# Weight splitting spread out and its copies put off by a step, the MLP begun three steps later, and the squares of the first chunk shared by two engines

## The chip, the core and the metric

The kernel runs on one core of a Trainium2 chip. The metric is device time in microseconds (us) of one execution. The engines named below are TensorE (PE; its weight loads are PEld), VectorE (DVE), ScalarE (ACT), GpSimd (POOL, which here only issues transfers) and SyncE (SP, which only issues transfers). Each engine runs its own instructions in the order in which the program gives them, and waits at the first whose operands or target are not ready.

## What is computed

```python
scores = (1.0 / S) * np.matmul(z, z.transpose(0, 2, 1))   # z: 4 x 3008 x 64
attn = np.maximum(scores, 0.0) ** 2
x = (u * np.matmul(attn, v)).reshape(B * S, D)            # u, v: 4 x 3008 x 256
h = x @ w_in                                              # 256 x 2048
g = h * np.clip(h + 3.0, 0.0, 6.0) / 6.0
y = g @ w_out                                             # 2048 x 256
```

All in float32; the two weights arrive as 64-bit floats.

## The kernel before, in words

**Precision.** Every operand of a matmul is split into a high part, rounded to the type that TensorE multiplies (a copy, cast or square, mostly on ScalarE), and a low part, the rest (a subtraction on VectorE). A product is then three matmuls: high by high, high by low, low by high.

**Steps.** A batch has 6 chunks of 512 columns (the last one 448), and a chunk takes 12 pairs of row tiles; one pass of the inner loop, numbered g from 0 to 287, is a *step* and handles one pair. In a step `attend` multiplies pair g with v (12 matmuls into the two banks o0 and o1), while `scores` prepares pair g + 2: four matmuls (s), two Relu evictions on ScalarE (L367), the square (`r2`), its rounded high part (`ah`) and its low part (`al`, L73). Scores are symmetric. A pair that was computed already for another chunk is read back from DRAM, transposed on VectorE (L318, `rm`) and split, which takes no score matmuls. I call such a pair mirrored and the others direct. Squares that a later chunk needs are written to DRAM by `keep`. In the first chunk the full-precision square is a VectorE multiplication (L384); in chunks 1 to 3 it is a second ScalarE square (L382). At a chunk's end two VectorE multiplications (L440) form x from u and the banks o0, o1.

**Weights.** `weight_ops` is a generator. For each of 16 weight blocks (in0, out0, in1, out1, ... out7) it decodes the 64-bit floats in seven VectorE operations (`to_f32`), for an "in" block forms four sums `s`, then queues ScalarE copies for the high parts into the tile `wb`, subtracts the low parts on VectorE (L73 wb) and writes `wb` to DRAM (L183, `dwin`, `dwout`). There is one buffer `wb`. `weight_work` takes `build_rate(g)` yields of the generator in each step, in `background()`. The queued copies are put into ScalarE's program by `flush_copies`, which `scores` and `from_mirror` call, and which the builder itself calls before its subtractions.

**MLP.** A *group* (m = 0 to 95) multiplies one block of x with one in/out block pair: 7 products of 3 matmuls (m; Strassen's scheme, tiles `ra`, `hb`, `rb`) and 24 matmuls (y). A group spans three steps, from step `MLP_FROM` on; the groups that are left after step 287 run back to back in a last loop. At its start a group reads block m + 1 of w_in and block m of w_out back from DRAM (`fetch_w`, L194: `wi`, `wo`). Its results are split into `gh0`, `gl0`, `gh1`, `gl1` of `gpool`, which nothing uses before the first group. `split_x` splits a block of x (6 VectorE low parts and sums of 512 or 1024 columns) in the three steps before the block's first group, and then `load_u` (L432) fetches the next u into the one buffer.

**Queues.** All hardware transfers are issued by SP in program order: `keep` (L304), reads of mirrored pairs (L287), weight writes (L183) and reads (L194), `load_u`. GpSimd issues the raw weights (L101, `wraw`).

Of the kernel before, what the change touches and what calls it, by code (L numbers as in the profile page):

```python
# [7 lines left out]
F32 = mybir.dt.float32  # L8
U32 = mybir.dt.uint32
F32R = mybir.dt.float32r  # L10
AF = mybir.ActivationFunctionType
ALU = mybir.AluOpType
# [3 lines left out]
P = 128  # L16
CH = 512
# [5 lines left out]
NFP = NF // 2  # L23
NPR = B * NCH // 2

MLP_FROM = 30
EVERY = 3
AFTER = MLP_FROM - 27

# [7 lines left out]
def relu2_attention_then_hswish_mlp(  # L37
# [9 lines left out]
    nc = tc.nc  # L47
# [18 lines left out]
    def f(ap):  # L66
        return ap.bitcast(F32)
# [4 lines left out]
    def sub(out, a, b):  # L72
        nc.vector.tensor_tensor(out=out, in0=a, in1=b, op=ALU.subtract)  # L73

    def add(out, a, b):
        nc.vector.tensor_tensor(out=out, in0=a, in1=b, op=ALU.add)  # L76
# [8 lines left out]
    wide = w_in.shape[-1] == 2 * DFF  # L85

    copies = []

    def flush_copies():
        while copies:  # L90
            copies.pop(0)()

    raws = {}

    def fetch_raw(kind, q):
        cols = slice(q * 2 * P, q * 2 * P + 2 * P) if kind == "in" else slice(0, D)
        src = w_in if kind == "in" else w_out[q * 2 * P:q * 2 * P + 2 * P]
        src = src.rearrange("(k p) f -> p k f", p=P)
        if wide:
            raw = rpool.tile([P, 2, D, 2], U32, tag="r", name="wraw")  # L100
            nc.gpsimd.dma_start(  # L101
                out=raw.rearrange("p k n w -> p k (n w)"),
                in_=src[:, :, 2 * cols.start:2 * cols.stop],
            )
        else:
            raw = rpool.tile([P, 2, D], F32, tag="r", name="wraw")
            nc.gpsimd.dma_start(out=raw, in_=src[:, :, cols])
        raws["w", kind, q] = raw
# [33 lines left out]
        return f0  # L142

    dw = {}

    def build(kind, q, then):

        raw = raws.pop(("w", kind, q))
        if wide:
            w = yield from to_f32(raw)  # L150
        else:
            w = raw
        then()
        if kind == "in":
            s = stg.tile([P, 4, P], F32, tag="stg", name="s4")
            t = wpool.tile([P, 2, 7, P], F32R, tag="wb", name="wb")
            a11, a21 = w[:, 0, :P], w[:, 0, P:]
            a12, a22 = w[:, 1, :P], w[:, 1, P:]
            add(s[:, 0], a21, a22)
            copies.append(lambda: nc.scalar.copy(out=t[:, 0, A11:A22], in_=w[:, :, :P]))  # L160
            copies.append(lambda: nc.scalar.copy(out=t[:, 0, A22], in_=a22))
            yield
            sub(s[:, 1], s[:, 0], a11)
            yield
            sub(s[:, 2], a11, a21)
            yield
            sub(s[:, 3], a12, s[:, 1])
            copies.append(lambda: nc.scalar.copy(out=t[:, 0, S1:], in_=s))
            yield
            flush_copies()  # L170
            sub(t[:, 1, A11:A22], w[:, :, :P], f(t[:, 0, A11:A22]))
            yield
            sub(t[:, 1, A22], a22, f(t[:, 0, A22]))
            yield
            sub(t[:, 1, S1:], s, f(t[:, 0, S1:]))
        else:
            t = wpool.tile([P, 2, 2, D], F32R, tag="wb", name="wb")
            copies.append(lambda: nc.scalar.copy(out=t[:, 0], in_=w))
            yield
            flush_copies()  # L180
            sub(t[:, 1], w, f(t[:, 0]))
        d = dw[kind, q] = dwpool.tile(list(t.shape), F32, tag=f"{kind}{q}", name=f"dw{kind}")
        nc.sync.dma_start(out=d, in_=f(t))  # L183
        yield

    def fetch_w(kind, q):
        while (kind, q) not in dw:
# [159 lines left out]

        return t.rearrange("p r n -> p (r n)").rearrange("p (q m e) -> p m q e", q=4, m=8)

    def scores(b, c, p, square_on_act=False, banks="xx"):  # L350


        if p // 2 < c:
            yield from from_mirror(b, c, p)
            return
        n = width(c)
        zx, zy = (z[:, :n] for z in zt[b, c])
        rt = rpool.tile([P, 2, CH], F32, tag="r", name="rt")
        rn = rt[:, :, :n]
        for r in range(2):  # L360
            s = ps.tile([P, CH], F32, tag=banks[r], name="s")
            j = 2 * p + r
            cols = slice((j % 4) * P, (j % 4) * P + P)
            zj = zt[b, j // 4][0][:, cols]
            mm(s[:, :n], zj, zy, True, False)
            mm(s[:, :n], zj, zx, False, True)
            nc.scalar.activation(out=rn[:, r], in_=s[:, :n], func=AF.Relu, scale=1.0 / S)  # L367
            if not r:
                yield
        ah = apool.tile([P, 2, CH], F32R, tag="ah", name="ah")  # L370
        al = apool.tile([P, 2, CH], F32R, tag="al", name="al")
        hn, ln = ah[:, :, :n], al[:, :, :n]
        keeps = p // 2 > c
        r2, r_of, r2_of, h_of, l_of = rn, rn, rn, f(hn), ln
        if keeps or not square_on_act:
            r2 = r2_of = rpool.tile([P, 2, CH], F32, tag="r", name="r2")[:, :, :n]
        if keeps:
            r_of, r2_of = in_order(rn), by_quadrant(r2)
            h_of, l_of = in_order(f(hn)), in_order(ln)
        if square_on_act:  # L380
            nc.scalar.activation(out=hn, in_=rn, func=AF.Square)
            nc.scalar.activation(out=r2_of, in_=r_of, func=AF.Square)  # L382
        else:
            nc.vector.tensor_tensor(out=r2_of, in0=r_of, in1=r_of, op=ALU.mult)  # L384
            nc.scalar.activation(out=hn, in_=rn, func=AF.Square)  # L385
        flush_copies()
        if keeps:
            keep(b, c, p, r2)
        yield
        if p < NPAIR - 1:  # L390
            sub(l_of, r2_of, h_of)
        else:
            first, second = (slice(0, 4), slice(4, 8)) if keeps else (0, 1)
            to = in_order(hn) if keeps else hn
            sub(l_of[:, first], r2_of[:, first], h_of[:, first])
            sub(to[64:128, second], r2_of[64:128, second], h_of[64:128, second])
        at[b, c, p] = (ah, al)
        yield
# [202 lines left out]
    def weight_ops():  # L601
        fetch_raw(*weights[0])
        yield
        for n, w in enumerate(weights):
            yield from build(*w, lambda: n + 1 < len(weights) and fetch_raw(*weights[n + 1]))

    w_ops = weight_ops()

    def build_rate(g):
        return 0 if g < 6 else 2 if g < 12 else 5 if g < MLP_FROM else 4  # L610

    def weight_work(n):
        for _ in range(n):
# [19 lines left out]
    with tc.manual_schedule():  # L633
# [16 lines left out]
        for i, (b, c) in enumerate(chunks):  # L650
            ahead = b + 1 if c == NCH - 1 and b + 1 < B else None
            for p in range(NPAIR):
                g = i * NPAIR + p
                pair = pairs[g]
                if i == 0:
# [6 lines left out]
                    if p % 2 == 0 and p // 2 + 2 < NCH:  # L662
                        split_z(0, p // 2 + 2)
                at_mlp, on = divmod(g - MLP_FROM, EVERY)
                if at_mlp < 0:
                    unit = iter(())
                elif on == 0:
                    unit = group(at_mlp)
                if g + 2 < len(pairs):
                    nxt = scores(*pairs[g + 2], square_on_act=0 < i < 4, banks="xy" if at_mlp < 0 else "yx" if on == 2 else "yy")  # L670
                else:
                    nxt = iter(())
                g_done = min(g + 3, len(pairs))
# [138 lines left out]
```

## Time and profile before

| | |
|---|---|
| three runs | 1972.79, 1974.31 (median), 1980.26 us |
| the profiled execution | 1977.08 us |
| its span, first to last instruction | 1975.3 us |
| mean granted TensorE clock | 0.994 |
| PE busy | 1911.7 us (97%), 8400 matmuls |
| DVE busy | 1520.2 us (77%) |
| ACT busy | 1195.8 us (61%) |

Busy time is what the profile counts as an instruction running; matmuls overlap one another, so a busy PE is not a PE at its peak. "Idle before" an instruction is the time in which its engine had nothing running, and the name behind the arrow is what ended it.

### The profile page before, as it was taken

The page shows a single profiled execution, that of the slowest core. Times are in us where ns is not written, and L with a number is a line of the kernel's source. Part 1 is how long each engine was busy: PE and PEld are TensorE (multiplying, and loading weights), DVE is VectorE, ACT ScalarE, POOL GpSimd, SP SyncE. Part 2 cuts the span into 40 slices and gives each one's busy share as a digit, 9 for nine tenths or more (in the row PEclk, how much of TensorE's full clock was granted, in tenths as well). Part 3 has the DMA queues.
Part 4 walks back from the last instruction along what each step waited for, and adds up shares of the span by engine and source line. Part 5 has one row for each costly group of instructions (what it writes and reads, how often), then busy time and mean ns, then how long its engine had stood idle before and what let it go on. Part 6 is the DMA issues. An engine that isn't in the chain of part 4 may idle for free.

```text
span 1975.3 us, 23141 instructions
## 1 busy us (share of the span) xinstructions
PE 1911.7 (97%) x8400; PEld 1578.3 (80%) x8400; DVE 1520.2 (77%) x1762; ACT 1195.8 (61%) x1632; POOL 54.2 (3%) x88
## 2 busy tenths in 40 slices
PE   7878999999999999999999999999999999999998
PEld 5656777888888888888888888888888888888877
DVE  7888897887767767887767776878876787787675
ACT  6566656566555655567655655557665565564565
POOL 1000000010000000011000000001000000000000
PEclk9998999999999999999999999999999999999999
DMA  7877667746544555675635546576455464557243
GB/s 190 230 205 230 173 200 202 194 150 185 177 131 123 160 154 146 186 194 142 213 113 149 163 126 167 139 197 181 139 183 143 139 182 123 152 161 196 85 145 117
DMA packets 416177, 325.02 MB, mean 165 GB/s; under 512 B 252608, under 2 KB 375488, under 8 KB 416064
## 3 DMA queue, kind: packets, MB, share of 16 engines
q1 hardware_dynamic: 408704, 299.96, 53.6%
q0 software_dynamic: 7360, 23.60, 4.3%
q8 instruction: 66, 1.08, 0.2%
q14 instruction: 47, 0.39, 0.1%
HBM read 239.34 MB, written 84.15 MB: 164 GB/s over the span
## 4 chain that ended last, share of the span: by engine, by line
PE 77%; DVE 10%; ACT 5%; DMA 5%; issue 3%; SPq 1%; DVEq 0%; ACTq 0%; POOLq 0%
PE o L70 29%; PE y L70 22%; PE m L70 20%; PE s L70 6%; DVE rm L318 1%; DVE r L384 1%; DMA l<-d 1%; DVE xl L73 1%; ACT rt L367 1%; DVE al L73 1%; DVE rb L541 1%; DMA wo<-dwout 1%; SPq L287 1%; DMA d<-r 1%; DMA wraw<-in_w_in_dram 1%
## 5 line engine op out<-in xcount | busy, mean ns | idle before, releaser
L70 PE MATMUL y<-gh,wo 128*128 128x512 f32 (+1 forms) x1536 | 531.0, 387 | 3.6 <-DMA wo<-dwout 3.6
L70 PE MATMUL m<-xh,wi 128*128 128x512 f32 (+1 forms) x1344 | 493.0, 389 | 12.9 <-ACT rt L367 5.8
L70 PE MATMUL o<-ah,vl 128*128 128x512 f32 (+1 forms) x1152 | 447.6, 389 | 10.9 <-DVE u L440 5.0
L70 PE MATMUL o<-ah,vh 128*128 128x512 f32 (+1 forms) x1152 | 446.5, 388 | 0.0
L70 PE MATMUL o<-al,vh 128*128 128x512 f32 (+1 forms) x1104 | 428.7, 388 | 9.3 <-DVE al L73 9.3
L70 PEld LDWEIGHTS y<-gh,wo 128*128 128x128 f32 x1536 | 288.8, 188 | 59.9 <-issue 3.3
L70 PEld LDWEIGHTS m<-xh,wi 128*128 128x128 f32 x1344 | 252.8, 188 | 73.2 <-ACT rt L367 10.4
L70 PE MATMUL y<-gl,wo 128*128 128x512 f32 (+1 forms) x768 | 298.0, 388 | 2.5 <-DVE gl L73 2.3
L367 ACT ACTIVATE rt<-s 128x512 f32<-128x512 f32 x336 | 195.5, 595 | 125.2 <-PE s L70 124.5
L384 DVE TENSOR_TENSOR r<-rt 128x1024 f32<-128x1024 f32 (+1 forms) x145 | 175.5, 1210 | 116.5 <-ACT rt L367 116.1
L70 PEld LDWEIGHTS o<-ah,vl 128*128 128x128 f32 x1152 | 217.7, 189 | 59.0 <-DVE u L440 4.9
L70 PE MATMUL m<-xl,wi 128*128 128x512 f32 (+1 forms) x672 | 260.3, 387 | 0.7 <-DVE xl L73 0.7
L70 PEld LDWEIGHTS o<-al,vh 128*128 128x128 f32 x1104 | 208.7, 189 | 52.9 <-DVE al L73 11.6
L70 PEld LDWEIGHTS o<-ah,vh 128*128 128x128 f32 x1152 | 217.5, 189 | 41.5
L76 DVE TENSOR_TENSOR hb<-hb,m 128x512 f32<-128x512 f32 (+1 forms) x192 | 129.1, 672 | 106.9 <-PE m L70 105.3
L573 ACT ACTIVATE ra<-m,three 128x512 f32<-128x512 f32 (+1 forms) x96 | 65.3, 681 | 218.9 <-PE m L70 210.1
L73 DVE TENSOR_TENSOR al<-r,ah 128x1024 fp32r<-128x1024 f32 (+2 forms) x163 | 185.1, 1136 | 12.0 <-ACT r L382 10.1
L70 PEld LDWEIGHTS y<-gl,wo 128*128 128x128 f32 x768 | 144.4, 188 | 33.9 <-DVE gl L73 6.9
L73 DVE TENSOR_TENSOR gl<-rb,gh 128x1024 fp32r<-128x1024 f32 (+1 forms) x96 | 115.3, 1201 | 55.1 <-ACT gh L80 54.0
L385 ACT ACTIVATE ah<-rt 128x1024 fp32r<-128x1024 f32 (+1 forms) x145 | 153.2, 1057 | 4.6
L70 PE MATMUL s<-zy,zx 128*128 128x512 f32 x336 | 134.3, 400 | 19.5 <-DVE zx L73 11.9
L70 PEld LDWEIGHTS m<-xl,wi 128*128 128x128 f32 x672 | 126.5, 188 | 23.5 <-DVE xl L73 1.0
(69 smaller groups left out, 2166.8 us busy)
## 6 DMA issues: line engine op xcount, KB each, us to landing
wi<-dwin SPq DMA_DIRECT2D x96, 896.0 KB, 5.9
d<-r SPq DMA_DIRECT2D x220, 256.0 KB, 3.3
wo<-dwout SPq DMA_DIRECT2D x96, 512.0 KB, 6.7
l<-d SPq DMA_DIRECT2D x320, 128.0 KB, 3.4
l<-d SPq DMA_DIRECT2D x160, 112.0 KB, 3.3
vraw<-in_v_dram POOLq DMA_DIRECT2D x33, 256.0 KB, 4.1
u<-in_ut_dram SPq DMA_DIRECT2D x8, 1024.0 KB, 5.5
out_dram<-y SPq DMA_DIRECT2D x16, 512.0 KB, 4.9
```

The source lines that it names most:

```text
L70: nc.tensor.matmul(out, lhsT=lhsT, rhs=rhs, start=start, stop=stop, skip_group_check=part)
L73: nc.vector.tensor_tensor(out=out, in0=a, in1=b, op=ALU.subtract)
L76: nc.vector.tensor_tensor(out=out, in0=a, in1=b, op=ALU.add)
L287: nc.sync.dma_start(out=t[32 * q:32 * q + 32, :nk, :], in_=src[:, c0:c0 + 64].rearrange("(k e) f -> e k f", e=32),)
L318: nc.vector.transpose(out=rn.rearrange("p r (k e) -> p r k e", e=32), in_=t[:, :n // 32].rearrange("p k (r e) -> p r k e", r=2),)
L367: nc.scalar.activation(out=rn[:, r], in_=s[:, :n], func=AF.Relu, scale=1.0 / S)
L384: nc.vector.tensor_tensor(out=r2_of, in0=r_of, in1=r_of, op=ALU.mult)
L385: nc.scalar.activation(out=hn, in_=rn, func=AF.Square)
L541: nc.vector.scalar_tensor_tensor(out=out, in0=out, scalar=6.0, in1=h, op0=ALU.min, op1=ALU.mult)
L573: nc.scalar.activation(out=ra[:, 1], in_=c21, func=AF.Relu, bias=three)
```

## The change

Four things are altered. (1) A queued copy remembers its step (`now`), and `flush_copies` puts it into ScalarE's program only in a later step; only `finish`, which subtracts the low parts, flushes everything. `finish` of a block now runs after the seven decode operations of the next block. (2) High and low part have a tile each and are written to DRAM by a transfer each. Until step 30 the blocks take turns on three pairs of tiles (`wh`/`wl`, and the idle `gh0`/`gl0` and `gh1`/`gl1`), from step 31 on all use `wh`/`wl`. (3) The MLP begins at step 33 and not 30, which moves `split_x` and `load_u` by three steps too and leaves 11 groups, not 10, for the last loop; the generator is called at other rates. (4) In the first chunk VectorE squares the first half of a pair and ScalarE the second ("da"); chunks 1 to 3 ("aa") and the rest ("dd") are as before.

```diff
@@ -23,7 +23,7 @@
 NFP = NF // 2
 NPR = B * NCH // 2
 
-MLP_FROM = 30
+MLP_FROM = 33
 EVERY = 3
 AFTER = MLP_FROM - 27
 
@@ -85,10 +85,15 @@
     wide = w_in.shape[-1] == 2 * DFF
 
     copies = []
-
-    def flush_copies():
-        while copies:
-            copies.pop(0)()
+    now = -1
+
+    def copy_later(out, of):
+        copies.append((now, out, of))
+
+    def flush_copies(upto=None):
+        while copies and (upto is not None or copies[0][0] < now):
+            _, out, of = copies.pop(0)
+            nc.scalar.copy(out=out, in_=of)
 
     raws = {}
 
@@ -142,46 +147,66 @@
         return f0
 
     dw = {}
-
-    def build(kind, q, then):
-
-        raw = raws.pop(("w", kind, q))
-        if wide:
-            w = yield from to_f32(raw)
+    early = True
+
+    def pieces(kind, w):
+
+        hi, lo = piece_tiles(kind)
+        if kind == "out":
+            copy_later(hi, w)
+            return [(hi, lo, w)]
+        s = stg.tile([P, 4, P], F32, tag="stg", name="s4")
+        a11, a21 = w[:, 0, :P], w[:, 0, P:]
+        a12, a22 = w[:, 1, :P], w[:, 1, P:]
+        copy_later(hi[:, A11:A22], w[:, :, :P])
+        copy_later(hi[:, A22], a22)
+        add(s[:, 0], a21, a22)
+        yield
+        sub(s[:, 1], s[:, 0], a11)
+        yield
+        sub(s[:, 2], a11, a21)
+        yield
+        sub(s[:, 3], a12, s[:, 1])
+        copy_later(hi[:, S1:], s)
+        yield
+        return [
+            (hi[:, A11:A22], lo[:, A11:A22], w[:, :, :P]),
+            (hi[:, A22], lo[:, A22], a22),
+            (hi[:, S1:], lo[:, S1:], s),
+            hi, lo,
+        ]
+
+    def finish(kind, q, parts):
+        if kind == "out":
+            hi, lo = parts[0][:2]
         else:
-            w = raw
-        then()
-        if kind == "in":
-            s = stg.tile([P, 4, P], F32, tag="stg", name="s4")
-            t = wpool.tile([P, 2, 7, P], F32R, tag="wb", name="wb")
-            a11, a21 = w[:, 0, :P], w[:, 0, P:]
-            a12, a22 = w[:, 1, :P], w[:, 1, P:]
-            add(s[:, 0], a21, a22)
-            copies.append(lambda: nc.scalar.copy(out=t[:, 0, A11:A22], in_=w[:, :, :P]))
-            copies.append(lambda: nc.scalar.copy(out=t[:, 0, A22], in_=a22))
+            *parts, hi, lo = parts
+        flush_copies(upto=now)
+        for h, l, of in parts:
+            sub(l, of, f(h))
             yield
-            sub(s[:, 1], s[:, 0], a11)
-            yield
-            sub(s[:, 2], a11, a21)
-            yield
-            sub(s[:, 3], a12, s[:, 1])
-            copies.append(lambda: nc.scalar.copy(out=t[:, 0, S1:], in_=s))
-            yield
-            flush_copies()
-            sub(t[:, 1, A11:A22], w[:, :, :P], f(t[:, 0, A11:A22]))
-            yield
-            sub(t[:, 1, A22], a22, f(t[:, 0, A22]))
-            yield
-            sub(t[:, 1, S1:], s, f(t[:, 0, S1:]))
-        else:
-            t = wpool.tile([P, 2, 2, D], F32R, tag="wb", name="wb")
-            copies.append(lambda: nc.scalar.copy(out=t[:, 0], in_=w))
-            yield
-            flush_copies()
-            sub(t[:, 1], w, f(t[:, 0]))
-        d = dw[kind, q] = dwpool.tile(list(t.shape), F32, tag=f"{kind}{q}", name=f"dw{kind}")
-        nc.sync.dma_start(out=d, in_=f(t))
-        yield
+        d = dw[kind, q] = dwpool.tile([P, 2, *hi.shape[1:]], F32, tag=f"{kind}{q}", name=f"dw{kind}")
+        for k, t in enumerate((hi, lo)):
+            nc.sync.dma_start(out=d[:, k], in_=f(t))
+
+    built = []
+
+    def piece_tiles(kind):
+        homes = (("wh", "wl"), ("gh0", "gl0"), ("gh1", "gl1")) if early else (("wh", "wl"),)
+        tags = homes[len(built) % len(homes)]
+        built.append(kind)
+        tiles = []
+        for tag in tags:
+            if tag[0] == "g":
+                t = gpool.tile([P, 2, CH], F32R, tag=tag, name=tag)
+                t = t.rearrange("p r n -> p (r n)")
+            else:
+                t = wpool.tile([P, 7 * P], F32R, tag=tag, name=tag)
+            if kind == "in":
+                tiles.append(t[:, :7 * P].rearrange("p (m f) -> p m f", m=7))
+            else:
+                tiles.append(t[:, :2 * D].rearrange("p (r d) -> p r d", r=2))
+        return tiles
 
     def fetch_w(kind, q):
         while (kind, q) not in dw:
@@ -347,7 +372,7 @@
 
         return t.rearrange("p r n -> p (r n)").rearrange("p (q m e) -> p m q e", q=4, m=8)
 
-    def scores(b, c, p, square_on_act=False, banks="xx"):
+    def scores(b, c, p, square_on="da", banks="xx"):
 
 
         if p // 2 < c:
@@ -372,17 +397,29 @@
         hn, ln = ah[:, :, :n], al[:, :, :n]
         keeps = p // 2 > c
         r2, r_of, r2_of, h_of, l_of = rn, rn, rn, f(hn), ln
-        if keeps or not square_on_act:
+        if keeps or square_on != "aa":
             r2 = r2_of = rpool.tile([P, 2, CH], F32, tag="r", name="r2")[:, :, :n]
         if keeps:
             r_of, r2_of = in_order(rn), by_quadrant(r2)
             h_of, l_of = in_order(f(hn)), in_order(ln)
-        if square_on_act:
-            nc.scalar.activation(out=hn, in_=rn, func=AF.Square)
-            nc.scalar.activation(out=r2_of, in_=r_of, func=AF.Square)
-        else:
-            nc.vector.tensor_tensor(out=r2_of, in0=r_of, in1=r_of, op=ALU.mult)
-            nc.scalar.activation(out=hn, in_=rn, func=AF.Square)
+
+        def square(on, rows):
+            to, of = (r2_of[:, rows], r_of[:, rows])
+            if on == "a":
+                nc.scalar.activation(out=to, in_=of, func=AF.Square)
+            else:
+                nc.vector.tensor_tensor(out=to, in0=of, in1=of, op=ALU.mult)
+
+        half = 4 if keeps else 1
+        if square_on[0] == square_on[1] == "d":
+            square("d", slice(None))
+        elif square_on[0] == "d":
+            square("d", slice(0, half))
+        nc.scalar.activation(out=hn, in_=rn, func=AF.Square)
+        if square_on[0] == "a":
+            square("a", slice(None))
+        elif square_on[1] == "a":
+            square("a", slice(half, None))
         flush_copies()
         if keeps:
             keep(b, c, p, r2)
@@ -601,13 +638,22 @@
     def weight_ops():
         fetch_raw(*weights[0])
         yield
-        for n, w in enumerate(weights):
-            yield from build(*w, lambda: n + 1 < len(weights) and fetch_raw(*weights[n + 1]))
+        before = None
+        for n, (kind, q) in enumerate(weights):
+            w = raws.pop(("w", kind, q))
+            if wide:
+                w = yield from to_f32(w)
+            if n + 1 < len(weights):
+                fetch_raw(*weights[n + 1])
+            if before:
+                yield from finish(*before)
+            before = kind, q, (yield from pieces(kind, w))
+        yield from finish(*before)
 
     w_ops = weight_ops()
 
     def build_rate(g):
-        return 0 if g < 6 else 2 if g < 12 else 5 if g < MLP_FROM else 4
+        return 1 if g < 12 else 3 if g < 18 else 4 if g < MLP_FROM else 5
 
     def weight_work(n):
         for _ in range(n):
@@ -662,12 +708,13 @@
                     if p % 2 == 0 and p // 2 + 2 < NCH:
                         split_z(0, p // 2 + 2)
                 at_mlp, on = divmod(g - MLP_FROM, EVERY)
+                early, now = g < MLP_FROM - 2, g
                 if at_mlp < 0:
                     unit = iter(())
                 elif on == 0:
                     unit = group(at_mlp)
                 if g + 2 < len(pairs):
-                    nxt = scores(*pairs[g + 2], square_on_act=0 < i < 4, banks="xy" if at_mlp < 0 else "yx" if on == 2 else "yy")
+                    nxt = scores(*pairs[g + 2], square_on="da" if i < 1 else "aa" if i < 4 else "dd", banks="xy" if at_mlp < 0 else "yx" if on == 2 else "yy")
                 else:
                     nxt = iter(())
                 g_done = min(g + 3, len(pairs))
```

## Rows read from the trace of the kernel before

**Rows 1.** The page's first part: busy time, share of the span, instructions.
```profile
PE 1911.7 (97%) x8400; PEld 1578.3 (80%) x8400; DVE 1520.2 (77%) x1762; ACT 1195.8 (61%) x1632; POOL 54.2 (3%) x88
```

**Rows 2.** Windows: start to end, length, busy (count) per engine, granted clock, DMA share, GB/s.
```profile
0.00:15.84 15.84, 3.98 (x9) 2.16 (x9) 8.16 (x11) 9.05 (x13) 4.50 (x12) 1.00 1.02 232
15.84:67.68 51.84, 48.85 (x198) 38.53 (x199) 44.72 (x56) 32.56 (x50) 1.46 (x2) 1.00 0.72 193
67.68:124.00 56.32, 44.67 (x182) 34.28 (x180) 46.58 (x76) 35.17 (x51) 4.26 (x6) 0.97 0.79 219
124.00:163.16 39.16, 27.76 (x97) 20.45 (x98) 33.74 (x53) 21.07 (x31) 1.42 (x2) 0.84 0.72 200
163.16:198.27 35.11, 33.83 (x143) 26.95 (x144) 29.68 (x43) 24.91 (x34) 1.42 (x2) 0.98 0.80 238
198.27:281.85 83.58, 81.29 (x351) 66.37 (x350) 71.68 (x102) 52.67 (x71) 2.85 (x4) 0.98 0.66 192
281.85:362.13 80.28, 75.94 (x331) 61.45 (x330) 66.49 (x78) 45.37 (x60) 1.98 (x3) 1.00 0.68 191
```

**Rows 3.** Chain of waits, 210 to 220 us: start, length, what.
```profile
214.31 1.36 PE m L70 x6
```

**Rows 4.** Waits of ScalarE, 45 to 330 us: total, times, longest.
```profile
ACT wb L178 <- DVE t L76: 13.7, 6, 4.7
ACT wb L168 <- DVE s L73: 9.9, 6, 2.9
ACT wb L160 <- DVE t L76: 6.4, 1, 6.4
ACT wb L160 <- DMA dwout<-wb: 6.1, 2, 3.4
```

**Rows 5.** Timeline of ScalarE and of PE, 82 to 88 us: start, length, instruction, idle before.
```profile
86.14 0.40 ACT L160 CAST wb<-t 128x256 fp32r<-128x256 f32 x1 [3.42 <-DMA dwout<-wb]
86.66 0.59 ACT L367 ACTIVATE rt<-s 128x512 f32<-128x512 f32 x1
...
87.30 0.50 PE L70 MATMUL s<-zy,zx 128*128 128x512 f32 x1 [2.25 <-ACT rt L367]
```

**Rows 6.** Waits of VectorE, 45 to 330 us.
```profile
DVE al L73 <- ACT r L382: 10.1, 5, 3.1
DVE t L115 <- DMA wraw<-in_w_in_dram: 3.2, 2, 2.0
DVE wb L73 <- ACT wb L178: 2.7, 4, 0.7
```

**Rows 7.** Groups by shape, whole span: count, busy, mean ns, idle before.
```profile
L384 DVE TENSOR_TENSOR r<-rt 128x1024 f32<-128x1024 f32 x137 | 166.8, 1217 | 115.3 <-ACT rt L367 114.9
L76 DVE TENSOR_TENSOR hb<-hb,m 128x512 f32<-128x512 f32 x128 | 87.4, 683 | 85.5 <-PE m L70 83.9
L80 ACT CAST vh<-vraw 128x512 fp32r<-128x512 f32 x48 | 29.2, 608 | 0.0
L73 DVE TENSOR_TENSOR s<-s,t 128x128 f32<-128x128 f32 x8 | 2.3, 286 | 0.2
```

**Rows 8.** Windows of one tile alone, wraw (DVE, POOL) and then wb (DVE, ACT).
```profile
0.00:340.00 340.00, 64.41 (x112) 11.42 (x16) 0.97 0.73 205
...
0.00:340.00 340.00, 15.66 (x32) 14.57 (x32) 0.97 0.73 205
```

**Rows 9.** Transfers, 30 to 310 us: count, KB each, median us to landing.
```profile
l<-d SPq DMA_DIRECT2D x76, 128.0 KB, 4.4
dwin<-wb SPq DMA_DIRECT2D x8, 896.0 KB, 5.0
```

**Rows 10.** Waits of SP's queue, 30 to 310 us, and one of PE.
```profile
SPq L287 <- DVE rm L318: 33.9, 5, 14.0
SPq L183 <- DVE wb L73: 14.2, 3, 10.5
SPq L194 <- DMA dwin<-wb: 7.0, 1, 7.0
...
PE y L70 <- DMA wo<-dwout: 2.9, 1, 2.9
```

## The prediction

> **What bounds the kernel now.** I first read the busy shares, then cut the span at the chunk ends, then asked who waited for whom in the disturbed part. TensorE is busy for 97% of the span [rows 1], so over the whole run it is the bound. Undisturbed, six matmuls take 1.36 us [rows 3], 0.2267 us each; all my TensorE work is counted at that price. The windows [rows 2] show where it falls short. Their edges are the second u multiplication of each chunk, 15.84 is the first matmul that depends on a full pipeline, 163.16 the first matmul of the MLP. The five chunk stretches, with TensorE's work counted from the code (16 matmuls a direct pair, 12 a mirrored one, 2 fewer at a chunk's end):
>
> A, steps 0 to 11, 51.8 us: 190 matmuls, 43.1 us; VectorE busy 44.7.
> B, steps 12 to 23, 56.3 us: 182, 41.3 us; VectorE 46.6.
> C, steps 24 to 35, 74.3 us (39.16 + 35.11): 240, 54.4 us; VectorE 33.74 + 29.68 = 63.4.
> D, steps 36 to 47, 83.6 us: 346, 78.4 us; VectorE 71.7.
> E, steps 48 to 59, 80.3 us: 338, 76.6 us; VectorE 66.5.
>
> Together 346.3 us against 293.8 us of matmul work: 52 us are lost here, and VectorE, not TensorE, is the longer one in A, B and C. That is the weight splitting. In 45 to 330 us ScalarE stood before the weights' copies for 13.7 + 9.9 + 6.4 us until VectorE had decoded, and for 6.1 us until the single `wb` had been written out [rows 4]. One such wait can be followed [rows 5]: a copy is held for 3.42 us, the Relu behind it runs at 86.66, and TensorE, which needs the bank that this Relu empties, stands until 87.30. In turn VectorE waited 10.1 us for ScalarE's second square (`al <- r`) [rows 6]. The clock adds to it: it was granted at 0.84 in the first part of C, where TensorE was broken up most, and at 1.00 in A and E [rows 2]; that cost is inside the stretches' times.
>
> **The change, part by part.** *Weight work.* Decode, low parts and sums cost VectorE 64.41 + 15.66 us [rows 8] and 32 small sums of 0.286 us [rows 7], 89.2 us in all. That amount stays; it is 185 yields of the generator before and 177 after, so 0.482 and 0.504 us a yield. By the two rates the stretches take 12, 60, 54, 48, 11 yields before and 12, 42, 51, 60, 12 after. VectorE's load changes by 0, -7.8, -0.3, +7.1 and +0.7 us.
>
> *First squares.* A full square is 1.217 us [rows 7]. Half of one I price at a 128x512 VectorE operation, 0.683 us, so VectorE saves 0.53 us in each of 12 pairs, 6.4 us in A. ScalarE gains 12 times 0.608 us (its 128x512 cast), 7.3 us: 32.6 becomes 39.9 us under TensorE's 43.1, hidden if nothing else delays ScalarE. If that cover fails, A keeps its old length; that is its upper bound.
>
> *MLP at step 33.* One group, 45 matmuls or 10.2 us, leaves C for the last loop, which TensorE bounds; there it costs its 10.2 us in full. C loses the same TensorE work and VectorE's share of a group, five operations of 0.683 and three of 1.22 us, 7.1 us.
>
> *Copies a step later, more tiles.* The copies themselves stay (14.57 us of ScalarE [rows 8]); the 36.1 us of waits in front of them should mostly go, and with them VectorE's 10.1. What is late next is VectorE itself in C, and in D both engines. `fetch_raw` comes 3 or 5 yields ahead of its decode instead of 2 or 7, so the 3.2 us wait for `wraw` [rows 6] should not grow. `finish` can still flush in the step in which it subtracts; that wait was 0.7 us at worst [rows 6].
>
> *Transfers.* Sixteen more writes pass through SP, and behind SP's own waits for VectorE [rows 10]. Nobody waits for them directly but the next user of the tile and `fetch_w`. At the end there is one new wait: block in7 is finished by yield 176, and at yield 177, in step 50, its two writes are issued and out7's copy and subtraction follow at once into the same `wh`/`wl`. ScalarE and VectorE then stand until the writes have landed. A half write lies between 4.4 us (128 KB) and 5.0 us (896 KB) [rows 9]; I take 5. Behind it queue the second square part, `al` of pair g + 2 and the Relu evictions; TensorE still has the step's last matmuls, so by the ratio in [rows 5], 2.25 of 3.42, some 3.3 us reach it. It replaces the waits of before in the same place, 7.0 us on SP's read of `wi` and 2.9 us on TensorE [rows 10]. Net about nothing; bounds -3 and +3.
>
> The rows give almost no difference between 128 and 896 KB, so halving a write shortens its landing little, and two writes in place of one carry the constant part twice. The Trainium skill ("DMA: Bandwidth & Descriptors", the anatomy of one DMA) says so too: about 2.0 us fixed per transfer plus bytes over 436 GB/s, fitted on GpSimd's path, and its rules advise to coalesce; no run here times such a half alone, and where rows have a duration I use that. By its figures a half write of 448 KB would land in an estimated 3.1 us, and the end of E would come out a good 1 us earlier than I take.
>
> *Start.* The first raw weights are asked for in step 0, not 6, where the transfer engines are full (share 1.02) at 232 GB/s [rows 2]: 512 KB take 2.3 us from the first loads, at worst. Two half squares come off VectorE ahead of 15.84, 1.1 us at best. Between +2.3 and -1.1 I take 0, since VectorE was the later one there.
>
> `load_u` now comes three steps ahead of its use and not six; three steps are 18 us or more in D (83.6 / 12 = 7.0 us each), so I cost it nothing. The first group needs `gh0` in step 35; the last early block in it is written out in step 26.
>
> **The sum.** A: VectorE 44.7 - 6.4 = 38.3, so TensorE's 43.1 bounds it, and I leave 3.9 of the 8.7 us that it lost before: 47. B: VectorE 38.8, TensorE 41.3; mirrored pairs are still locally VectorE's, 46. C: VectorE 63.4 - 0.3 - 7.1 = 56.0; of its 10.9 us idle about half stay: 61.5. D: VectorE 78.8 and TensorE 78.4, both full; between no change (83.6) and VectorE's work plus its old 11.9 idle (90.7) the middle, 87. E: the old length plus 0.7: 81.0. Together 322.5, that is 23.8 less; minus the 10.2 us given back at the end, 13.6 us gained. The profiled execution takes 1977.1 us and would take 1963.5; it lies 2.8 us above the median, so on the median's footing 1974.3 - 13.6 = **1961 us**.
>
> **Rivals.** *Bigger gain.* With ScalarE free every stretch could fall to its longer engine: 43.1, 41.3, 56.0, 78.8, 76.6, sum 295.8, which is 50.5 less and 40 after the group: 1934. For it speaks that the waits named in [rows 4, 6] are mostly of ScalarE and VectorE for each other around the copies; against it that in D two engines would have to be full at once. Half of the way is 1948.
>
> *The idle time stays.* VectorE's waits may move to other partners. With the old idle of each stretch on top of the new VectorE load: A 47, B 48.5, C 66.9, D 90.7, E 81.0, sum 334.1, less by 12.2; minus 10.2 leaves 2.0: 1972. For it speaks that delaying MLP work does not help a stretch that VectorE bounds, and that D gets 7.1 us more of it.
>
> *The one pair of tiles, slower.* From step 31 the nine blocks out3 to out7 share `wh`/`wl`, and each copy comes one step behind the write of the block before. If SP reaches the write late (its waits for VectorE reach 14.0 and 10.5 us [rows 10]), ScalarE stands at each. With 5.0 us a copy and the ratio of [rows 5], 0.66, passed on, 9 x 5.0 x 0.66 = 30 us: 1991. It turns the result slower than 1984 from 23 / 9 / 0.66 = 3.9 us a copy on. Against it: the high part's write needs no VectorE result, and a step of 7 us covers 5.0.
>
> **Chances and range.** A change under 0.5%, 9.9 us, is about what a measurement of this kernel cannot tell from none. Forecast (1953 to 1964) 0.46; bigger gain, below 1953, 0.13; idle stays, mostly 1964 to 1984, 0.28; one pair, above 1984, 0.13. So faster 0.59, same 0.28, slower 0.13. The range leaves out the one pair and the far part of the bigger gain, some 0.18: 1946 to 1977.
>
> **What would show it.** In the profile after, ScalarE's waits before the weights' copies fall from 36 us to under 10. A ends near 62 us and B near 108; the MLP begins near 152 with the clock at 1.00 in most of A to C. VectorE is over 90% busy in C and D, and D is longer than before. In step 50 a copy and a subtraction for out7 wait for `dwin`. The last loop has 11 groups. I am wrong if C and D together lose more than B and A gain, which the `wh` copies' waits, or a slower A with ScalarE ahead of TensorE's waits, would show.

## The result, and the profile after

The changed kernel takes 1954.22 us (median of 4 runs, 1953.07 to 1955.31) where the kernel before takes 1976.08 (4 runs): a ratio of 0.9888 with a 95% interval of 0.9867 to 0.9910. That is 1.1% less, 1 lies outside the interval, and 1954 lies inside the range. The gain is 22 us; I had forecast 13.6.

The first part of the page after, to be read against [rows 1]: the same 8400 matmuls, now 98% of a span of 1952.6 us.

```profile
PE 1905.4 (98%) x8400; PEld 1576.2 (81%) x8400; DVE 1511.2 (77%) x1762; ACT 1202.8 (62%) x1646; POOL 54.2 (3%) x88
```

The windows of the same chunks, to be read against [rows 2] (columns as there). Their edges are again the second u multiplication of each chunk; 16.16 is the first matmul of A, 142.91 the first matmul of the MLP.

```profile
0.00:16.16 16.16, 3.98 (x9) 2.16 (x9) 7.08 (x11) 10.09 (x15) 5.25 (x13) 1.00 1.02 250
16.16:63.10 46.94, 46.94 (x192) 38.00 (x193) 37.86 (x56) 36.87 (x59) 0.73 (x1) 1.00 0.72 203
63.10:106.98 43.88, 42.59 (x187) 34.64 (x185) 39.25 (x61) 37.64 (x52) 2.86 (x4) 1.00 0.91 233
106.98:142.91 35.93, 31.09 (x130) 24.68 (x131) 34.78 (x54) 23.70 (x33) 2.13 (x3) 0.98 0.99 251
142.91:166.38 23.47, 20.07 (x73) 14.87 (x72) 20.70 (x33) 15.55 (x23) 1.42 (x2) 0.88 0.84 254
166.38:249.72 83.34, 80.00 (x345) 63.91 (x343) 77.77 (x116) 52.13 (x70) 3.56 (x5) 1.00 0.77 213
249.72:328.39 78.67, 75.23 (x328) 61.30 (x329) 67.42 (x80) 46.15 (x62) 2.00 (x3) 1.00 0.70 193
```

A, B and C have become shorter by 4.9, 12.4 and 14.9 us (51.8, 56.3 and 74.3 before), E by 1.6, and D, which carries 12 yields of weight work more, is as long as it was. Together 312.2 us for 346.3. The rest of the span pays the moved group back, as these two windows show, the first of the kernel before, the second of the changed one: 11.0 us more.

```profile
362.13:1975.30 1613.17, 1595.34 (x7098) 1328.08 (x7096) 1219.11 (x1352) 975.00 (x1327) 36.28 (x57) 1.00 0.55 156
```

```profile
328.39:1952.60 1624.21, 1605.45 (x7142) 1336.69 (x7140) 1226.30 (x1360) 980.66 (x1335) 36.30 (x57) 1.00 0.55 156
```

The waits of ScalarE and of VectorE after, 45 to 330 us (total, times, longest). Of the four rows in [rows 4], 36.1 us, one is left with 5.4, and VectorE's wait for the second square is 6.0 where [rows 6] has 10.1:

```profile
ACT wh L96 <- DMA dwin<-wh: 5.4, 3, 2.4
```

```profile
DVE al L73 <- ACT r L409: 6.0, 10, 1.1
...
DVE wl L73 <- DMA dwin<-wl: 4.1, 2, 2.7
```

The stall that was forecast for step 50 is there. Timelines of ScalarE, VectorE, SP and TensorE after, 261 to 275 us (start, length, instruction, idle before): the write of in7's high part is issued at 261.81, that of its low part at 267.34, and out7's copy and subtraction wait for the two.

```profile
268.89 0.62 ACT L96 CAST wh<-t 128x512 fp32r<-128x512 f32 x1 [2.38 <-DMA dwin<-wh]
...
269.96 0.69 DVE L73 TENSOR_TENSOR wl<-t,wh 128x512 fp32r<-128x512 f32 x1 [2.65 <-DMA dwin<-wl]
...
261.81 1.89 SPq L190 DMA_DIRECT2D dwin<-wh  x1
267.34 0.34 SPq L190 DMA_DIRECT2D dwin<-wl  x1
...
273.91 0.50 PE L70 MATMUL m<-xh,wi 128*128 128x512 f32 x1 [0.50 <-ACT rt L392]
```

In A TensorE no longer stands: it is busy for 46.94 of 46.94 us. What A has above the 43.1 us of matmul work is mostly a slow start. The first 14 matmuls of A begin some 0.43 us apart, the later ones 0.23, though the row of A gives a granted clock of 1.00 (timeline of TensorE after).

```profile
16.16 0.79 PE L70 MATMUL s<-zy,zx 128*128 128x512 f32 x1 [6.06 <-DVE zx L73]
16.75 0.63 PE L70 MATMUL s<-zx 128*128 128x512 f32 x1
17.18 0.63 PE L70 MATMUL o<-ah,vl 128*128 128x512 f32 x1
...
22.73 0.39 PE L70 MATMUL s<-zy,zx 128*128 128x512 f32 x1
22.95 0.39 PE L70 MATMUL s<-zx 128*128 128x512 f32 x1
```

The number of such slow matmuls differs between the profiles below, from 6 to 14, so A by itself is uncertain by some 1.6 us (8 times 0.2): f1, whose program is the same until step 50, has 6 of them and an A of 45.5.

### The profile page after: what moved, and what is told of

Its sections match the earlier page's. It is cut to its first block, busy times and chain, and to the rows that moved or that the text cites. A ratio compares the mean times of both kernels' runs of the same rounds, so it can differ in the third digit from the quotient of the medians.

```text
span 1952.6 us, 23168 instructions
## 1 busy us (share of the span) xinstructions
PE 1905.4 (98%) x8400; PEld 1576.2 (81%) x8400; DVE 1511.2 (77%) x1762; ACT 1202.8 (62%) x1646; POOL 54.2 (3%) x88
## 4 chain that ended last, share of the span: by engine, by line
PE 82%; DVE 7%; DMA 4%; ACT 4%; issue 2%; SPq 1%; DVEq 0%; ACTq 0%
PE o L70 32%; PE y L70 22%; PE m L70 20%; PE s L70 7%; DMA l<-d 2%; DMA wo<-dwout 1%; DMA d<-r 1%; DVE rb L578 1%; SPq L312 1%; DVE xl L73 1%; DVE rm L343 1%; ACT rt L392 1%; DVE ra L578 1%; DVE al L73 1%; DVE gl L73 1%
## 5 line engine op out<-in xcount | busy, mean ns | idle before, releaser
L411 DVE TENSOR_TENSOR r<-rt 128x1024 f32<-128x1024 f32 (+2 forms) x145 | 168.0, 1159 | 108.4 <-ACT rt L392 108.0
L418 ACT ACTIVATE ah<-rt 128x1024 fp32r<-128x1024 f32 x168 | 177.6, 1057 | 5.4
```

What stands on the lines that cost most here:

```text
L411: nc.vector.tensor_tensor(out=to, in0=of, in1=of, op=ALU.mult)
```

## The experiments

Twelve kernels ran, in three groups. Times are medians; the kernel before took 1975.2, 1975.9 and 1975.2 us beside the three groups. The lengths of the five stretches come from the timeline of each profile (from the ninth matmul, then from one second u multiplication to the next); "copies" is ScalarE's idle time in front of the weights' copies there.

| run | us | ratio, 95% interval | A | B | C | D | E | copies |
|---|---|---|---|---|---|---|---|---|
| before | 1976.1 | | 51.8 | 56.3 | 74.3 | 83.6 | 80.3 | 36.1 |
| changed | 1954.2 | 0.9867 to 0.9910 | 46.9 | 43.9 | 59.4 | 83.3 | 78.7 | 5.4 |
| e1_dd_first | 1956.2 | 0.9884 to 0.9921 | 48.8 | 43.1 | 59.4 | 82.8 | 79.0 | 5.3 |
| e2_flush_now | 1973.4 | 0.9975 to 0.9998 | 46.6 | 43.9 | 64.2 | 96.2 | 81.0 | 37.3 |
| e3_finish_now | 1971.3 | 0.9963 to 0.9986 | 46.3 | 46.6 | 60.6 | 96.4 | 78.7 | 29.4 |
| e4_one_pair | 1960.3 | 0.9901 to 0.9942 | 45.7 | 48.2 | 58.4 | 83.1 | 79.0 | 15.0 |
| e5_mlp30 | 1958.6 | 0.9896 to 0.9921 | 46.4 | 43.9 | 66.5 | 84.0 | 86.7 | 11.0 |
| e6_old_rates | 1973.4 | 0.9980 to 0.9998 | 47.4 | 51.5 | 66.7 | 89.1 | 78.4 | 11.2 |
| b2_rates_mlp33 | 1971.3 | 0.9965 to 0.9985 | 50.1 | 45.0 | 63.5 | 86.9 | 85.0 | 41.6 |
| b1_da_only | 1975.4 | 0.9987 to 1.0004 | 46.7 | 56.0 | 74.1 | 83.5 | 83.5 | 35.0 |
| f1_end_apart | 1953.3 | 0.9866 to 0.9896 | 45.5 | 43.9 | 59.1 | 83.7 | 77.9 | 3.3 |
| f2_old_rates_end_apart | 1964.8 | 0.9929 to 0.9956 | 47.3 | 51.8 | 66.4 | 81.0 | 76.1 | 4.7 |
| f3_mlp30_end_apart | 1952.8 | 0.9866 to 0.9893 | 46.4 | 43.9 | 66.5 | 84.1 | 80.1 | 6.2 |
| g1_earlier_weights | 1962.8 | 0.9925 to 0.9948 | 46.5 | 49.2 | 72.7 | 83.1 | 80.2 | 16.0 |

The five stretches explain the whole: against the changed kernel their sum and the span of the same profile change alike within 2.5 us in every run (with 10 us off for a run that begins the MLP at step 30). With copies at once they add 19.7 us, and the median is 19.2 longer.

### The four parts undone one by one

**e1_dd_first: the first squares back on VectorE**

```diff
-square_on="da" if i < 1 else "aa" if i < 4 else "dd"
+square_on="aa" if 0 < i < 4 else "dd"
```

> The changed kernel with the first chunk's squares all on VectorE again; all else as changed (1954 us). My theory, that in the first chunk the longer engine sets the time: VectorE goes from 37.9 to about 44.5 us in stretch A, above TensorE's 43.1, so A (46.9 us) grows by 3 to 5 us and the whole ends near 1958. Rival, that the look-ahead of two steps absorbs VectorE's surplus: A and the whole stay within 1 us of the changed kernel.

A grew by 1.9 us and B gave 0.8 back; the whole is 2.0 longer, which the two intervals do not tell apart. VectorE has 44.4 us in A there, and TensorE stands for 2.0 us of it where it stood for none. The direction is that of the longer engine. The size looks like half of what I expected, but this profile has 7 of the slow matmuls where the changed kernel has 14; from an equal start A would be some 3.3 us longer, an estimate from 7 times 0.2 us.

**e2_flush_now: the copies in the step that queues them**

```diff
-while copies and (upto is not None or copies[0][0] < now):
+while copies:
```

> The changed kernel with the queued copies put into ScalarE's program in the step that queues them, as before; low parts still after the next decode, three tile pairs, new rates. My theory, that ScalarE's waits in front of the copies cost the time: they come back to 20 us or more, stretches B and C (43.9 and 59.4) grow by some 8 us together, the whole is near 1962. Rival, that the lower rate in B did it: waits or not, B and C grow by under 2 us and the whole stays within 2 us of 1954.

The loss is 19 us, twice what I expected, and in another place: A and B do not change at all, C grows by 4.8 and D by 12.9 us. The waits of ScalarE in that run, 45 to 330 us, are no longer for VectorE's decode but for the writes:

```profile
ACT wh L96 <- DMA dwin<-wh: 15.9, 3, 8.8
ACT wh L96 <- DMA dwout<-wh: 15.4, 3, 5.8
```

One of them, in timelines of SP, ScalarE and TensorE of the same run: the high part's write is issued at 182.65, the next block's copy stands for 8.84 us until it has landed, and behind that copy in ScalarE's order are the eviction and the rounding that the y matmuls need.

```profile
182.65 2.88 SPq L190 DMA_DIRECT2D dwin<-wh  x1
...
189.63 0.62 ACT L96 CAST wh<-t 128x512 fp32r<-128x512 f32 x1 [8.84 <-DMA dwin<-wh]
190.16 0.68 ACT L610 ACTIVATE ra<-m,three 128x512 f32<-128x512 f32 x1
191.59 1.04 ACT L616 CAST gh<-ra 128x1024 fp32r<-128x1024 f32 x1 [0.76 <-DVE ra L578]
...
192.69 0.80 PE L70 MATMUL y<-gh,wo 128*128 128x512 f32 x1 [3.91 <-ACT gh L616]
```

The new order ends one block and begins the next in the same yield, so without the delay the copies from step 31 on meet writes that have just been issued. 31.9 us more of such waits cost 19.7 us, a ratio of 0.62; [rows 5] had given 0.66. That the two are so near is partly chance, for the 19.7 us hold more than waits. The window of D shows it: TensorE, broken up like this, was granted a mean clock of 0.94 (1.00 in the changed kernel). Of D's 12.9 us more, 6.8 are time in which TensorE had nothing running, and in 6.1 its matmuls were busy for longer (353 in the record, where the changed kernel has 345).

```profile
170.34:266.52 96.18, 86.07 (x353) 68.39 (x351) 78.00 (x115) 52.30 (x71) 3.56 (x5) 0.94 0.66 185
```

**e3_finish_now: the low parts right behind the sums**

```diff
-            if before:
-                yield from finish(*before)
-            before = kind, q, (yield from pieces(kind, w))
-        yield from finish(*before)
+            yield from finish(kind, q, (yield from pieces(kind, w)))
```

> The changed kernel with a block's low parts right behind its sums, before the next decode; finish then also flushes the copies at once, so both halves of the postponement are undone, with three tile pairs and the new rates kept. My theory: the same as with the copies alone undone, plus VectorE's wait for each copy (0.7 us at 16 blocks): near 1964. Rival, that the order of the low parts matters by itself: over 5 us more than with the copies alone undone.

1971.3, not longer than e2 but 2 us shorter: the rival falls, and my own number, near 1964, missed as well. Here seven decode operations lie between a write and the next copy again, so no copy waits for a write; the copies wait for the decode instead (rows of ScalarE's waits, 45 to 330 us), and D comes out the same, 96.4.

```profile
ACT wh L96 <- DVE t L76: 13.5, 5, 4.9
...
ACT wh L96 <- DVE s L73: 7.3, 4, 2.6
ACT gh L96 <- DVE t L76: 6.4, 3, 2.5
```

**e4_one_pair: one pair of tiles**

```diff
-homes = (("wh", "wl"), ("gh0", "gl0"), ("gh1", "gl1")) if early else (("wh", "wl"),)
+homes = (("wh", "wl"),)
```

> The changed kernel with one pair of tiles (wh, wl) throughout. My theory: only copies that come right behind a write wait; before, with one buffer, that was 6.1 us in two waits, here 7 blocks more come one step behind a write, each wait under 2 us and mostly hidden: the whole within 3 us of 1954. Rival, that the tile pairs carry the gain: ScalarE waits of 3 us and more at each early block, B and C together up by 8 us or more, 1962.

The median is 6 us longer, but the six runs lie between 1955.4 and 1966.3 and the profile is of the shortest, only 1 us above the changed kernel; so I can say that the tile pairs are worth 1 to 12 us, and no more. The median lies between my theory's 1957 at most and the rival's 1962. In the profile the copies wait 9.6 us more, for writes, and it is B that loses (48.2); the five stretches together lose only 2.1, a ratio of 0.22, so what such a wait costs is no constant.

### Rates, start of the MLP, and the old kernel's side

**e5_mlp30: the MLP at step 30**

```diff
-MLP_FROM = 33
+MLP_FROM = 30
-4 if g < MLP_FROM else 5
+4 if g < 33 else 5
```

> The changed kernel with the MLP begun at step 30 as before; the rates stay tied to the step numbers (5 from step 33), and the shared tile pair begins with step 28. My theory, that VectorE bounds stretch C: a group moved back into C costs C VectorE's 7.1 us and its latencies, 8 to 11 us, and saves 10.2 us in the last loop: the whole within 2.5 us of 1954. Rival, that the later start is what made room for the weights: C grows by 15 us or more and the whole is 1960 or over.

Both missed: C grew by 7.1 us only, less than the 10.2 saved, but E by 8.0, and nearly all of that is one stall of TensorE:

```profile
267.52 0.79 PE L70 MATMUL m<-xh,wi 128*128 128x512 f32 x1 [7.93 <-ACT ra L590]
```

It stands behind out7's copy, which waits for in7's write (ScalarE's timeline of that run). That is the meeting of step 50, harder and earlier: group 6, which reads block in7, begins in step 48 here and takes the generator's yields up to it at once.

```profile
266.36 0.62 ACT L96 CAST wh<-t 128x512 fp32r<-128x512 f32 x1 [4.92 <-DMA dwin<-wh]
266.89 0.58 ACT L590 COPY ra<-m 128x512 f32<-128x512 f32 x1
```

**e6_old_rates and f2_old_rates_end_apart**

```diff
-return 1 if g < 12 else 3 if g < 18 else 4 if g < MLP_FROM else 5
+return 0 if g < 6 else 2 if g < 12 else 5 if g < MLP_FROM else 4
```

> The changed kernel with the old rates of weight work (0, 2 from step 6, 5 from step 12, 4 from the MLP on). After the first four runs I hold that the rates and the postponement need each other: the lower rate earns A and B, and the postponement lets D carry the higher one. Then here B has VectorE's 46 us again, near 49, C near 62, D falls to some 80: the whole 1958 to 1962. Rival, that the postponement alone is the gain and the rates are indifferent: within 2 us of 1954.

B and C were 2 and 5 us longer than I expected (51.5, 66.7), and D went the other way (89.1 for 80). The weights end in step 47 there, and out7's copy meets in7's write just ahead of the chunk's u multiplication. SP issues that write only at 261.52, behind eight reads of mirrored pairs (timelines of SP, ScalarE and TensorE):

```profile
249.67 11.76 SPq L312 DMA_DIRECT2D l<-d  x8
261.52 0.43 SPq L190 DMA_DIRECT2D dwin<-wh  x1
...
267.65 0.62 ACT L96 CAST wh<-t 128x512 fp32r<-128x512 f32 x1 [9.51 <-DMA dwin<-wh]
...
271.01 0.79 PE L70 MATMUL o<-ah,vl 128*128 128x512 f32 x1 [8.75 <-DVE u L477]
```

That run mixed two things, so I ran it again with the last `finish` put apart:

```diff
+        for _ in range(7):
+            yield
         yield from finish(*before)
```

> The old rates again, with the last finish put apart. In the run with the old rates TensorE stood 8.9 us for the u multiplication behind out7's copy at the end of D, so that run mixed two things. My theory: that stall alone goes, D falls from 89.1 to about 81, A, B and C stay at 47, 51 and 67, the whole is 1962 to 1966, and the new rates are worth 8 to 12 us beside the postponement. Rival, that the rates are indifferent: 1954 to 1957.

As expected: D 81.0, the whole 1964.8. Beside the postponement the new rates are worth 11.5 us (against f1 below, which has the end put apart too), and the windows of B and C of this run show where: VectorE, with 47.47 and 58.66 us, is the longest engine in both.

```profile
62.96:114.73 51.77, 43.47 (x185) 33.73 (x183) 47.47 (x79) 39.07 (x56) 4.31 (x6) 1.00 0.95 255
114.73:181.10 66.37, 52.64 (x201) 40.23 (x202) 58.66 (x92) 39.04 (x55) 3.56 (x5) 0.90 0.79 221
```

**b2_rates_mlp33: the kernel before with the new rates and MLP_FROM = 33 alone**

```diff
-MLP_FROM = 30
+MLP_FROM = 33
-return 0 if g < 6 else 2 if g < 12 else 5 if g < MLP_FROM else 4
+return 1 if g < 12 else 3 if g < 18 else 4 if g < MLP_FROM else 5
```

> The kernel before with only the new rates and the MLP at step 33; copies at once, one buffer wb, squares as before. If rates and postponement need each other: A near 49 and B near 47 as in the changed kernel, but D near 96 as in the two runs with copies at once, so the whole falls by only 1 to 4 us, 1971 to 1974. Rival, that the lower rate in B carries the gain: D stays at 84 to 87 and the whole is near 1960.

1971.3, a gain of 4.5 us only, as the first theory has it. B fell to 45.0. But C, D and E take 235.3 us, only 2.8 less than before though a group of 10 us has left them; the changed kernel takes 221.4. D alone is 86.9, near the rival's 87 and not 96, so the theory had the loss in the wrong place: C has 4.1 us more than the changed kernel, D 3.5, and E, which still has 20 of 185 yields to do, 6.3. The copies' waits in that run, 45 to 330 us, are mostly the old ones:

```profile
ACT wb L178 <- DVE t L76: 15.6, 5, 4.5
ACT wb L168 <- DVE s L73: 10.1, 6, 2.7
ACT wb L160 <- DVE t L76: 9.2, 4, 3.7
```

**b1_da_only: the kernel before with the first squares shared**

```diff
+elif share:
+    nc.vector.tensor_tensor(out=r2_of[:, :half], in0=one, in1=one, op=ALU.mult)
+    nc.scalar.activation(out=hn, in_=rn, func=AF.Square)
+    nc.scalar.activation(out=r2_of[:, half:], in_=two, func=AF.Square)
```

> The kernel before with only the first chunk's squares shared. VectorE's 44.7 us in A fall by 6.4: if A is set by its longer engine, A (51.8) falls by 3 to 5 us and the whole by 2 to 4, near 1972. Rival, that A's losses are the weights' burst at rate 2 from step 6 on, so that the squares change nothing: under 1 us.

A did what the theory asks, 51.8 to 46.7 with VectorE at 38.2 us. The whole did what the rival asks: 1975.4, no difference from before. In the profile E is 3.2 us longer, and the timeline of TensorE shows where. It stood for a block of w_out that was read back, 3.49 us where the kernel before stood 2.88, and the 13 matmuls from there on began some 0.43 us apart, where before they went on at 0.23. The granted clock of that window is 0.68; before it was 1.00 in the window behind the stall. Whether the executions that were not profiled lost their gain in the same way is not shown. The first row below is the stall and the second the window of this run; the third and fourth are the same of the kernel before.

```profile
296.86 0.76 PE L70 MATMUL y<-gh,wo 128*128 128x512 f32 x1 [3.49 <-DMA wo<-dwout]
296.00:306.00 10.00, 9.14 (x29) 7.36 (x30) 4.19 (x4) 3.68 (x5) 0.00 (x0) 0.68 0.59 125
...
302.09 0.47 PE L70 MATMUL y<-gh,wo 128*128 128x512 f32 x1 [2.88 <-DMA wo<-dwout]
302.00:312.00 10.00, 9.91 (x44) 8.26 (x45) 6.07 (x7) 5.83 (x8) 0.00 (x0) 1.00 0.73 158
```

The squares are what brings VectorE under TensorE in A. The new rates alone do not: A has 12 yields at either rates, and without the shared squares VectorE has 44.4 us there (e1, b2).

### Towards a faster version

**f1_end_apart** is the changed kernel with the seven empty yields above.

> The changed kernel with seven empty yields before the last finish, so that out7's copy comes at least a step after in7's writes. My theory from the profile after: the wait of ScalarE and VectorE in step 50 (2.4 and 2.7 us) goes, of which TensorE saw 0.7: the whole within 1.5 us of 1954. Rival, my forecast's ratio of 0.66 for such waits: 1.7 us and the later waits with it, 1951 to 1952.

1953.3, as expected: 1 us less than the changed kernel and not told apart from it. The stall of step 50 costs little.

**f3_mlp30_end_apart** has MLP_FROM = 30 as well.

> The changed kernel with the MLP at step 30 and the last finish put apart. With the MLP at step 30 E had one stall of 8.1 us behind the end of the weights. My theory: that stall was the whole loss of the early start; without it C's 7 us more are less than the 10.2 saved in the last loop, and the whole is 1949 to 1952, under the changed kernel. Rival, that the weights are simply late (group 6 in step 48 takes six yields at once before it can start): E keeps a stall of 5 us or more and the whole is 1955 to 1959.

The stall in E shrank from 7.9 to 2.4 us and E from 86.7 to 80.1. 1952.8 is just outside what I expected and the same as f1: the early start itself is worth 1 us or nothing, since C pays 7 of the 10 us that the last loop saves, and E, with the stall that is left, 2.

**g1_earlier_weights** takes more weight work in A and B:

```diff
+return 1 if g < 8 else 2 if g < 12 else 4 if g < 33 else 5
```

> As the run before, with two yields a step in steps 8 to 11 and four in steps 12 to 17, so that the last block read back is ready before group 6 asks for it. My theory: A has 9 us of VectorE free, so A stays within 1 us of 47; B, where VectorE gets 3 us more and comes to 42 of 44, grows by 1 to 2; C keeps its length or loses a little; E has no stall: the whole 1947 to 1951, the fastest of all. Rival, that B is already set by VectorE: B grows by 3 us or more and the whole is no better than the run before.

Wrong: 1962.8. B grew by 5.3 us, as the rival has it, and C by 6.2 beyond f3. Whether VectorE's load or the waits of the copies did more of it, one run can't tell. Copies of blocks on the shared pair met fresh writes again, for 15.8 us in three waits; the worst one, with what stood behind it on ScalarE and at TensorE (timelines):

```profile
151.92 0.62 ACT L96 CAST wh<-t 128x512 fp32r<-128x512 f32 x1 [6.29 <-DMA dwin<-wh]
152.44 0.58 ACT L603 COPY hb<-m 128x512 f32<-128x512 f32 x1
...
153.08 0.80 PE L70 MATMUL m<-xh,wi 128*128 128x512 f32 x1 [7.18 <-ACT hb L603]
```

So no run beats the changed kernel by more than can be measured.

## Why the prediction was right, and where it was off

**VectorE's load by stretch** was right within 1.1 us: 38.3, 38.8, 56.0, 78.8 and 67.2 forecast, 37.9, 39.3, 55.5, 77.8 and 67.4 in the windows after. So was the moved group, 10.2 forecast and 11.0 found. Of the signs, ScalarE's waits under 10 us, the ends of A and B (63.1 and 107.0) and VectorE over 90% busy in C and D came true. A, 47 and 46.9, agrees in part by luck: I left 3.9 us of lost time there without saying what it was, TensorE lost none by standing, and 2.8 are the slow start (14 times 0.2), which is 1.2 in f1. The MLP began at 143 and not near 152, and the clock was granted at 1.00 in A and B and fell, to 0.88, only in the end of C, where [rows 2] have 0.84 for a longer stretch.

**The idle time on top of the load** was the term that I sized wrongly. I took 46, 61.5, 87 and 81 us for B to E; they are 43.9, 59.4, 83.3 and 78.7. D is the largest error: I went half of the way to VectorE's old idle of 11.9 us, and VectorE was idle for 5.6. "D is longer than before" was wrong. Together with A these come to 10.3 us. Of that the moved group took 0.8 back and the start 0.3, and the rest is what lies between the 13.6 forecast and the 22.7 us between the two profiled executions. So the mechanism held and the size did not: the measured time is 7 us under the forecast of 1961, near the edge of the bigger gain at 1953.

**The copies a step later** were right as a mechanism: the waits fell from 36.1 to 5.4 us. I had put their worth into B and C, through the waits of [rows 4]. The runs place it elsewhere. With the new rates and three tile pairs A and B are the same with or without the delay (e2), and C to E are 20 us longer without it; in the order of the kernel before they are 14 us longer (b2). What the delay buys is that C to E can carry their weight work. B's 12 us come mostly from the rates: 8 where the delay is there (f2, with the old rates, has B at 51.8), 11 where it is not (b2, 45.0). Neither part alone gains as much as both. Rates with the later MLP on the kernel before gain 4.5 us (b2); the postponement, tiles, squares and later MLP with the old rates gain 2.5 (e6), or 10.4 when the end is put apart (f2); all together gain 22, with the end put apart or not. By b2, f2 and f1 some 7 of the 22 us need both, an estimate from 21.9 - 10.4 - 4.5.

**The stall in step 50** is there, at 2.4 and 2.7 us and not 5, and TensorE stood 0.5 us for it, not 3.3; f1, without it, is 1 us shorter. I had both writes begin together. The high part's needs no VectorE result, as I had said myself under the rival, and SP issued it 5.5 us ahead of the low part's. Two other runs show that the price depends on when SP reaches the write and on what stands behind the copy: at the end of a chunk TensorE stood 8.8 us (e6), ahead of a group's first product 7.9 (e5).

**The rivals.** "The idle time stays" asked for 48.5 in B and 90.7 in D and is refuted by 43.9 and 83.3. "One pair of tiles" did not come about in the changed kernel, with 5.4 us of waits. e2 shows what such waits would do: without the delay ScalarE stood before six copies for their tile's writes, 31.3 us or 5.2 each, and the price is 19 us where I had nine waits of 5.0 and 30 us. "Bigger gain" asked for every stretch at its longer engine; each stayed 2 to 4.5 us above that, 16.4 together, so the truth lies between it and the forecast.

**The later MLP** I had priced as neutral but for what C gains. f3 against f1 says the same: no difference that can be measured.

## What to carry to other kernels

Where an engine works in order, a helper's copy that waits for another engine or for a write delays everything behind it; putting such a copy into the program one step after its inputs, and looking at what was written last to its target, can be worth more than its own time (here 19 us for copies that take 14.6). Then see which stretch has room on the engine that the helper loads, and move the work there: here each half alone gained 2 to 10 us, and both 22. Look at the last item of a software pipeline by itself, for there the step that hid its wait is missing.

## What the runs showed of the chip

Halving a write shortened its landing little: over all blocks the median from issue to landing is 4.2 us after (2.0 to 7.4) and was 5.0 before (2.6 to 7.5). The kinds of block differ. The transfers of the changed kernel, 30 to 310 us (count, KB each, median us to landing), are the first four rows; the last is `dwout` of the kernel before, whose `dwin` is in [rows 9]. For an "out" block 256 KB took 3.3 us where 512 KB had taken 5.7 (two early blocks in the other tiles took 5.3 and 5.9). For an "in" block 448 KB took 6.3 and 3.5 us where 896 KB had taken 5.0. Why the first of an "in" block's two writes is so slow is open.

```profile
dwin<-wh SPq DMA_DIRECT2D x6, 448.0 KB, 6.3
dwin<-wl SPq DMA_DIRECT2D x6, 448.0 KB, 3.5
dwout<-wh SPq DMA_DIRECT2D x6, 256.0 KB, 3.3
dwout<-wl SPq DMA_DIRECT2D x6, 256.0 KB, 3.3
...
dwout<-wb SPq DMA_DIRECT2D x8, 512.0 KB, 5.7
```

The Trainium skill ("DMA: Bandwidth & Descriptors", the anatomy of one DMA) would give an estimated 3.1 us for each 448 KB by its fit for one transfer. The second of the two writes is near that and the first far above it; the transfer engines were 77% to 99% busy in B to D, and the measurement decides.
